# Sorting the first four units in groups of four rows, and the third expert's weights behind the first slots' loads

## Chip, cores and metric

The kernel runs on one core of one Trainium2 chip. The metric is the device time of one execution in microseconds (us). The program is built once; input and output lie in the chip's memory.

## What is computed

A causal depthwise convolution with seven taps per head, softmax-normalised, over 8 x 3584 rows of 192 numbers; then a mixture of eight experts that sends each of the 28,672 rows to its best expert alone.

```python
out = np.einsum('hk,bskhg->bshg', w, x_unf)      # w: softmax of the 7 taps
logits = x @ w_gate                              # x: those 28672 rows
e_idx = np.argmax(logits, axis=1)
eom = 1.0 / (1.0 + np.exp(-(x @ w_output_gate)))
...
h = np.maximum(x[mask] @ w1[e], 0.0)             # 192 -> 1024
ye = h @ w2[e]                                   # 1024 -> 192
out[mask] = gate_w[mask, None] * eom[mask, e, None] * ye
```

## The kernel before

The rows are cut into 16 **units** of 1,792. For each unit `front_a` computes the convolution (PE, line 381, with the matrices `band`), transposes the result (line 404) and takes the logits (line 416, in tiles of 32 columns). `front_b` finds each row's expert on DVE and sorts: the unit is cut into 8 groups of 224 rows (112 on the lower and 112 on the upper block, `l`), and the rows of a group that go to one expert are packed into pieces of `QR` = 2 rows, the last piece of an expert padded. The sorting is a matmul with a selection matrix `pm` (DVE, line 519): four matmuls of line 558 per group write 128 pieces of two rows to PSUM, ACT copies them as fp16 to one of twelve buffers `xs` (line 358, through `evac`), and one indirect DMA of GpSimd, the **scatter** (`scatter`, line 574), writes the 128 pieces of 1 KB to places `du` (line 541) in the DRAM stream `xcg_sorted`, where each expert has its stretch. A group is so one PE step, one ACT copy and one scatter; a unit is eight of them.

The experts run over **slots** of 512 rows of the stream (`Slot`): SP loads a slot with two transposing DMAs, `xa` and `xb` (lines 689 and 691, `slot_load`), PE computes `first` (lines 733 and 741, out to `ht`) and, one slot later, `second` (line 790), ACT scales to `y`, and GpSimd scatters 128 rows a time to the output (line 594). There are 56 planned slots and 5 that choose their expert at run time; a loop behind them takes what is left over.

The weights of expert `e` are four DMAs of GpSimd's queue, cast to fp16 on the way into `wres` (`load_w`, line 339; in this order 256, 64, 64 and 384 KB of fp16). `first` needs the first three of them, `second` the fourth. Experts 0 and 1 are asked for at the start.

The order of the work is written out by hand. In the **fill** a string of letters gives it: `a` to `e` are steps of `front_a` of units 0 to 4, `0` to `3` steps of `front_b` of units 0 to 3, `W` one DMA of the third expert's weights (index 2), `L` the loads of the first three slots (SP's queue) with the four pieces of unit 5's `x`. After each letter the scatters that are ready go to GpSimd's queue. Behind the string come the **stages**, each with three or four slots, one unit's sorting and one unit's convolution, woven together; here experts 3 to 7 are loaded, one DMA at a time, at fixed places. The first slots need the scatters of units 0 and 1 complete. The last eight groups of unit 3 are sorted in the first stage. Slots take the experts in turn, so slot 7 is the first of expert 6 and slot 8 of expert 7.

GpSimd works its queue in order: a scatter, a weight DMA and an output scatter wait for whatever stands ahead.

Of the kernel before, what the change touches and what calls it, by code (L numbers as in the profile page):

```python
# [21 lines left out]
def kernel(  # L22
# [10 lines left out]
    nc = tc.nc  # L33
# [3 lines left out]
    E = moe_w1.shape[0]  # L37
# [35 lines left out]
    xcgq = xcg.rearrange("(a b) w -> a (b w)", b=QR)  # L73
# [165 lines left out]
    nc.vector.tensor_copy(out=hole, in_=rowi[:, 3:4])  # L239
    nc.vector.tensor_scalar(out=hole, in0=hole, scalar1=float(HB), scalar2=-64.0,  # L240
# [24 lines left out]
    NXS = 12  # L265
    xss = [const.tile([128, QR, RW], FP16, name=f"xs{i}") for i in range(NXS)]
    for t in xss:
        nc.gpsimd.memset(t[:, :, XW:RW], 0.0)

    poi = const.tile([128, QR, 128], U32)  # L270
    nc.gpsimd.iota(poi, pattern=[[1, QR], [QR, 128]], base=1, channel_multiplier=0)
    pos16 = const.tile([128, 256], FP16)
    nc.vector.tensor_copy(out=pos16, in_=poi.rearrange("p r j -> p (r j)"))

# [32 lines left out]
    c0 = NB * E  # L307
# [5 lines left out]

# [123 lines left out]
    def front_b(u, split=False):  # L437
        cv, gb = units.pop(u)
        P = slice(0, BP)
        mx = pr.tile([128, NB], FP32, tag="mx", name="mx")  # L440
# [35 lines left out]
        nc.vector.tensor_scalar(out=nu, in0=pn[:, 0:1], scalar1=float(QR - 1), scalar2=None,  # L476
                                op0=ALU.add)
        nc.vector.tensor_scalar(out=nu, in0=nu, scalar1=QR.bit_length() - 1, scalar2=None,
# [19 lines left out]
        nc.tensor.matmul(pk[:, 0:c0], np16, lsum[:, 0:c0], start=False, stop=False)  # L498
        nc.tensor.matmul(pk[:, c0:NK], np16, lsum[:, c0:NK], start=False, stop=True)
# [13 lines left out]
        def prep(i):  # L513
            if cv is not None and i % 2 == 0:
                for k in (i, NG + i):
                    nc.vector.tensor_copy(out=xr[P, k:k + 2, 0:D], in_=cv[P, k:k + 2, :])
            pms[i] = pp16.tile([128, 2, 256], FP16, tag="pm", name="pm")
            for l in range(2):
                nc.vector.tensor_scalar(out=pms[i][P, l, :], in0=pos16[P],  # L519
                                        scalar1=pos[P, l * NG + i:l * NG + i + 1],  # L520
                                        scalar2=None, op0=ALU.is_equal)
# [4 lines left out]
        if split:  # L526
# [10 lines left out]
            scalar=rowf[:, 0:1], in1=dd, op0=ALU.is_le, op1=ALU.mult)  # L537
# [3 lines left out]
        nc.vector.tensor_scalar(out=du, in0=dst, scalar1=rowf[:, 0:1], scalar2=None, op0=ALU.add)  # L541
# [3 lines left out]
        for i in range(NG):  # L545
            if i == 1 and u >= U0 and u != UA:
                v = u if u < UA else u - 1
                plans[v] = plan(v)
            if i + 2 < NG:
                prep(i + 2)  # L550
            while len(pend) >= NXS:
                emit_in()
            xs = xss[nxs[0] % NXS]
            nxs[0] += 1
            ps = pft()
            for r in range(QR):
                for l in range(2):
                    nc.tensor.matmul(ps[:, r * XW:(r + 1) * XW],  # L558
                                     pms[i][P, l, r * 128:(r + 1) * 128],
                                     xr[P, l * NG + i, :],  # L560
                                     start=(r == 0 and l == 0), stop=(r == QR - 1 and l == 1))
# [453 lines left out]
```

## Time and profile before

| | |
|---|---|
| runs | 549.5, 549.5, 551.89 us (median 549.5) |
| profiled execution | 549.7 us, its span 547.7 us |
| busy PE / DVE / ACT / POOL | 512.5 / 370.8 / 390.1 / 400.7 us |
| granted TensorE clock, mean | 0.977 |
| DMA | 91.28 MB, mean 167 GB/s |

The span is what the profile covers; 2.0 us of the execution lie outside it. Busy time is an engine's own; engines work beside one another. Idle time of an engine is listed by what ended it.

### The profile page before, as it was taken

The page shows a single profiled execution, that of the slowest core. Times are in us where ns is not written, and L with a number is a line of the kernel's source. Part 1 is how long each engine was busy: PE and PEld are TensorE (multiplying, and loading weights), DVE is VectorE, ACT ScalarE, POOL GpSimd, SP SyncE. Part 2 cuts the span into 40 slices and gives each one's busy share as a digit, 9 for nine tenths or more (in the row PEclk, how much of TensorE's full clock was granted, in tenths as well). Part 3 has the DMA queues.
Part 4 walks back from the last instruction along what each step waited for, and adds up shares of the span by engine and source line. Part 5 has one row for each costly group of instructions (what it writes and reads, how often), then busy time and mean ns, then how long its engine had stood idle before and what let it go on. Part 6 is the DMA issues. An engine that isn't in the chain of part 4 may idle for free.

```text
span 547.7 us, 16348 instructions
## 1 busy us (share of the span) xinstructions
PE 512.5 (94%) x5718; PEld 355.4 (65%) x5718; DVE 370.8 (68%) x1428; ACT 390.1 (71%) x754; POOL 400.7 (73%) x447
## 2 busy tenths in 40 slices
PE   8999799968999999999999999999999997999990
PEld 3666466745676766767776776777677774666660
DVE  7888768766686958677785867769587752565230
ACT  3897567746777777778777777877777785777750
POOL 8557876778677777777777777777777777777761
PEclk9999799998999999999999999999999999999995
DMA  8997999999987636957667685957373444679610
GB/s 149 288 300 244 172 222 188 204 175 236 194 197 150 180 116 136 213 118 173 173 141 198 141 214 123 199 138 164 100 145 95 119 106 115 143 157 249 206 66 19
DMA packets 154643, 91.28 MB, mean 167 GB/s; under 512 B 104009, under 2 KB 145588, under 8 KB 154560
## 3 DMA queue, kind: packets, MB, share of 16 engines
q1 hardware_dynamic: 127040, 43.76, 40.8%
q0 software_dynamic: 23360, 43.32, 31.8%
q10 hardware_dynamic: 4160, 3.15, 2.0%
q8 instruction: 45, 0.74, 0.6%
q14 instruction: 38, 0.31, 0.2%
HBM read 37.99 MB, written 42.07 MB: 146 GB/s over the span
## 4 chain that ended last, share of the span: by engine, by line
PE 69%; DMA 13%; DVE 5%; ACT 4%; issue 3%; SPq 2%; POOL 2%; POOLq 0%; ACTq 0%; DVEq 0%
PE pyt L790 23%; PE pp L733 17%; PE pp L741 10%; PE pf L381 6%; PE pf L558 6%; PE pf L404 4%; DMA xcg_sorted<-xs,du 4%; PE pf L416 3%; DMA out_dram<-y,oi 3%; DMA xb<-xcg_sorted 3%; DMA wres<-in_moe_w_dram 2%; DMA xt<-in_x_dram 2%; DVE ht L762 1%; POOL xcg_sorted L574 1%; ACT ht L764 1%
## 5 line engine op out<-in xcount | busy, mean ns | idle before, releaser
L594 POOL DMA_INDIRECT out_dram<-y,oi x236 | 234.5, 994 | 77.6 <-issue 40.8
L764 ACT ACTIVATE ht<-pp 128x1024 f16<-128x1024 f32 (+1 forms) x183 | 175.6, 994 | 47.6 <-PE pp L733 38.3
L790 PEld LDWEIGHTS <-ht 128*128 128x128 f16 x1888 | 160.5, 98 | 26.4 <-issue 1.3
L790 PE MATMUL pyt<-wres,ht 128*128 128x192 f16 x1792 | 177.2, 247 | 0.0
L574 POOL DMA_INDIRECT xcg_sorted<-xs,du x128 | 129.1, 1008 | 50.0 <-ACT xs L358 15.4
L762 DVE TENSOR_SCALAR ht<-pp 128x1024 f16<-128x1024 f32 (+1 forms) x61 | 72.5, 1188 | 93.2 <-PE pp L733 91.9
L798 ACT ACTIVATE y<-pyt,g 128x192 f32<-128x192 f32 x236 | 87.0, 424 | 35.2 <-PE pyt L790 27.7
L733 PE MATMUL pp<-xa,wres 128*128 128x512 f16 x224 | 89.2, 398 | 2.5 <-DMA xa<-xcg_sorted 2.5
L733 PE MATMUL pp<-xb,wres 128*128 128x512 f16 x224 | 86.3, 385 | 0.3 <-DMA xb<-xcg_sorted 0.3
L741 PE MATMUL pp<-xb,wres 64*128 64x512 f16 x224 | 70.7, 394 | 12.5 <-DMA wres<-in_moe_w_dram 7.2
L733 PEld LDWEIGHTS <-wres 128*128 128x128 f16 x448 | 41.4, 118 | 56.1 <-issue 31.8
L358 ACT CAST xs<-pf 128x392 f16<-128x392 f32 x128 | 63.2, 509 | 11.3 <-PE pf L558 10.7
L741 PE MATMUL pp<-xa,wres 64*128 64x512 f16 x224 | 70.9, 395 | 0.0
L558 PE MATMUL pf<-xrow,pm 120*128 120x196 f16 x512 | 63.9, 249 | 0.1
L519 DVE TENSOR_SCALAR pm<-pos,pos 120x256 f16<-120x256 f16 x256 | 63.9, 317 | 0.0
L381 PE MATMUL pf<-xt,band 64*64 64x192 f32 x896 | 49.5, 334 | 0.3 <-DMA xt<-in_x_dram 0.3
L358 ACT COPY tt<-pf 128x448 f32<-128x448 f32 x57 | 29.6, 554 | 26.4 <-PE pf L404 24.8
L358 ACT COPY cv<-pf 120x384 f32<-120x384 f32 x84 | 38.3, 508 | 14.0 <-PE pf L381 12.0
L558 PEld LDWEIGHTS <-pm 120*128 120x128 f16 x512 | 44.3, 98 | 4.7 <-DVE pm L519 1.0
L741 PEld LDWEIGHTS <-wres 64*128 64x128 f16 x448 | 17.3, 118 | 42.9 <-issue 33.9
L359 DVE COPY cv<-pf 120x384 f32<-120x384 f32 x44 | 24.4, 554 | 23.8 <-PE pf L381 23.4
L404 PEld LDWEIGHTS pf<-identf,cv 56*128 56x128 f32 x768 | 31.8, 142 | 10.9 <-DVE dd L535 2.6
(161 smaller groups left out, 512.6 us busy)
## 6 DMA issues: line engine op xcount, KB each, us to landing
xt<-in_x_dram SPq DMA_DIRECT2D x39, 384.0 KB
wd<-wres SPq DMA_DIRECT2D x5, 768.0 KB
out_dram<-y,oi POOLq DMA_INDIRECT x236
wres<-in_moe_w_dram POOLq DMA_DIRECT2D x8, 384.0 KB
wres<-in_moe_w_dram POOLq DMA_DIRECT2D x8, 256.0 KB
xcg_sorted<-zrow SPq DMA_DIRECT2D x8, 256.0 KB
xcg_sorted<-xs,du POOLq DMA_INDIRECT x128
xt<-in_x_dram SPq DMA_DIRECT2D x5, 336.0 KB
```

The lines of the kernel that those rows point to most:

```text
L358: return nc.scalar.copy(out=o, in_=i)
L381: nc.tensor.matmul(pcs[g][64 * c:64 * c + 64, o:o + NB // 2 * GH], band[64 * g:64 * g + 64, h + hh, :], xt[64 * g:64 * g + 64, c * NB // 2 ...
L519: nc.vector.tensor_scalar(out=pms[i][P, l, :], in0=pos16[P], scalar1=pos[P, l * NG + i:l * NG + i + 1], scalar2=None, op0=ALU.is_equal)
L558: nc.tensor.matmul(ps[:, r * XW:(r + 1) * XW], pms[i][P, l, r * 128:(r + 1) * 128], xr[P, l * NG + i, :], start=(r == 0 and l == 0), stop= ...
L574: i = nc.gpsimd.indirect_dma_start(out=xcgq, out_offset=bass.IndirectOffsetOnAxis(ap=du[:, i:i + 1], axis=0), in_=xs.rearrange("p r w -> p ...
L594: i = nc.gpsimd.indirect_dma_start(out=out, out_offset=bass.IndirectOffsetOnAxis(ap=oi[:, j:j + 1], axis=0), in_=y[:, j, :], in_offset=Non ...
L733: nc.tensor.matmul(pps[r][:, l, :], w[:, o:o + F // 2].rearrange("p (c q) -> p q c", q=FCH // 2)[:, 2 * q2 + r], x, start=(r == lead), sto ...
L741: nc.tensor.matmul(pps[r][:, l, :], w[p0:p0 + 64, F:WA].rearrange("p (c q) -> p q c", q=FCH // 2)[:, 2 * q2 + r], x[p0:p0 + 64], start=(r ...
L762: nc.vector.tensor_relu(out=ht, in_=pps[r])
L764: nc.scalar.activation(out=ht, in_=pps[r], func=AF.Relu)
L790: nc.tensor.matmul(self.pp[:, o:o + D], self.ht[fc // 2][:, fc % 2, q * 128:(q + 1) * 128], self.w[:, w:w + D], start=(fc == 0 and q % 2 = ...
L798: nc.scalar.activation(out=self.y[:, j, :], in_=self.pp[:, (j - j0) * D:(j - j0 + 1) * D], func=AF.Identity, scale=self.g[:, j:j + 1])
```

## The change

Units 0 to 3 (`u < UQ`) are sorted in pieces of four rows, the others in pieces of two as before. With pieces of four a group has at most 64 pieces, so two groups (`t`) share one buffer pair and one scatter of 128 pieces of 2 KB. In the fill the two groups are computed at once, each in one half of PE's columns, by eight matmuls a group in the place of four; unit 3, which is sorted in the first stage, keeps four matmuls a group, and each group's result is copied in two copies of 64 partitions. `du` takes three DVE instructions for such a unit in the place of one. The twelve buffers become one tile `xsb`. In the string the four `W` move from ahead of the `L` to behind it.

```diff
+    UQ = 4
...
+        q, ls, row = (2 * QR, lsum4, rowq) if u < UQ else (QR, lsum, rowf[:, 0:1])
...
-        nc.vector.tensor_scalar(out=du, in0=dst, scalar1=rowf[:, 0:1], scalar2=None, op0=ALU.add)
+        if q == QR:
+            nc.vector.tensor_scalar(out=du, in0=dst, scalar1=row, scalar2=None, op0=ALU.add)
+        else:
+            for g in range(2):
+                h = slice(64 * g, 64 * g + 64)
+                nc.vector.tensor_scalar(out=du[h, 0:NG // 2],
+                                        in0=dst[h].rearrange("p (t g) -> p g t", g=2)[:, g, :],
+                                        scalar1=row[h], scalar2=None, op0=ALU.add)
+            nc.vector.tensor_scalar(out=du[:, 0:NG // 2], in0=du[:, 0:NG // 2], scalar1=1,
+                                    scalar2=None, op0=ALU.logical_shift_right)
...
+            if fill[0] is None:
...
+                xq = xs[64 * g:64 * g + 64, :, 0:XW].rearrange("p (h r) w -> p r h w", r=2)
+                for r in (g, 1 - g):
+                    w = evac(xq[:, r], ps[64 * r:64 * r + 64, 0:2 * XW].rearrange(
+                        "p (h w) -> p h w", h=2), "dve" if g and r == 0 else "act")
...
+            else:
+                for r in range(2):
+                    for l in range(2):
+                        for j in range(2):
+                            nc.tensor.matmul(
+                                ps[64 * j:64 * j + 64, r * XW:(r + 1) * XW],
+                                pms[2 * t + j][P, l, (2 * g + r) * 64:(2 * g + r + 1) * 64],
+                                xr[P, l * NG + 2 * t + j, :],
+                                start=(r == 0 and l == 0), stop=(r == 1 and l == 1),
+                                tile_position=(0, 64 * j))
+                evac(xs[:, 2 * g:2 * g + 2, 0:XW],
+                     ps[:, 0:2 * XW].rearrange("p (r w) -> p r w", r=2), "act")
+            if g:
+                pend.append(lambda t=t, xs=xs: scatter(u, du[:, t:t + 1], xs, q))
...
-    for k in ("aaaaaaaapXbpab0bb00bb00brb00brcc00101c1c101X0c0ccq1dc1qcd1d2d212"
-              "1d21d1212dWW2Wtdde2We3L2e33223et223"):
+    for k in ("aaaaaaaapXbpab0bb00bb00brb00brcc00101c1c101X0c0ccq1dc1qcd1d2"
+              "d2121d21d1212d2tdde2e3LW2We3W3223Wet223"):
```

GpSimd's queue in the fill, from the last four scatters of unit 1 to the first weight DMA of the first stage (expert 3's, `128x2x512`), before (`xs` are the buffers, `xrow` the unit's two columns of gate weights):

```order
L574 DMA xcg_sorted<-xs_267,du 117504x512
L574 DMA xcg_sorted<-xs_268,du 117504x512
L339 DMA wres<-in_moe_w_dram 128x2x512
L339 DMA wres<-in_moe_w_dram 64x512
L574 DMA xcg_sorted<-xs_269,du 117504x512
L339 DMA wres<-in_moe_w_dram 64x512
L574 DMA xcg_sorted<-xs_270,du 117504x512
L339 DMA wres<-in_moe_w_dram 128x2x768
L574 DMA xcg_sorted<-xs_271,du 117504x512
L491 CAST xrow_257<-gs 120x16
```

and now, the last scatters of unit 1 and the first of unit 2 as `x3`:

```order
L619 DMA xcg_sorted<-xsb,du 58752x1024 x3
L338 DMA wres<-in_moe_w_dram 128x2x512
L619 DMA xcg_sorted<-xsb,du 58752x1024
L338 DMA wres<-in_moe_w_dram 64x512 x2
L491 CAST xrow_259<-gs 120x16
L492 TENSOR_TENSOR xrow_259<-gs,xrow_259 120x16
L619 DMA xcg_sorted<-xsb,du 58752x1024
L338 DMA wres<-in_moe_w_dram 128x2x768
L619 DMA xcg_sorted<-xsb,du 58752x1024
L338 DMA wres<-in_moe_w_dram 128x2x512
```

In the first fence the row ending in `xs_267` is unit 1's last scatter, and four more scatters of unit 2 stand behind the last row shown. On this queue there are half as many scatters, and the four weight DMAs still stand among unit 2's: the first behind two of its groups (before: one), the next two behind four (one and two), the fourth behind six (three). The `L` issues on SP's queue, whose order is the same in both.

PE's queue, the first of unit 0's groups: before, four matmuls for a group,

```order
L416 MATMUL pf<-tt,wg 32x224 x12
L558 LDWEIGHTS pm
L558 MATMUL pf<-xrow_256,pm 128x196
L558 LDWEIGHTS pm
L558 MATMUL pf<-xrow_256,pm 128x196
```

and now eight, in half-width pairs (`64x196`: 64 columns of the array, 196 rows through it):

```order
L415 MATMUL pf<-tt,wg 32x224 x12
L600 LDWEIGHTS pm
L600 MATMUL pf<-xrow_258,pm 64x196
L600 LDWEIGHTS pm
L600 MATMUL pf<-xrow_258,pm 64x196
L600 LDWEIGHTS pm
L600 MATMUL pf<-xrow_258,pm 64x196
```

Each matmul brings its own weight load, so units 0 to 2 issue 192 matmuls and as many loads where they issued 96.

## Rows read from the trace of the kernel before

**Rows 1.** Waits of PE: line, what for, us in total, times, longest.
```profile
PE pp L741 <- DMA wres<-in_moe_w_dram: 7.2, 2, 4.5
```
**Rows 2.** Timeline of PE, 50 to 136 us: start us, us, what, [idle before <-releaser].
```profile
50.22 0.51 PE L558 MATMUL pf<-xrow,pm 120*128 120x196 f16 x4
50.66 1.34 PE L416 MATMUL pf<-tt,wg 128*32 128x224 f32 x24
...
58.51 1.00 PE L558 MATMUL pf<-xrow,pm 120*128 120x196 f16 x8
63.46 0.58 PE L741 MATMUL pp<-xb,wres 64*128 64x512 f16 x1 [3.95 <-DMA xb<-xcg_sorted]
...
72.03 0.38 PE L741 MATMUL pp<-xb,wres 64*128 64x512 f16 x1 [0.95 <-DMA xb<-xcg_sorted]
...
122.28 0.40 PE L741 MATMUL pp<-xb,wres 64*128 64x512 f16 x1 [4.53 <-DMA wres<-in_moe_w_dram]
...
134.63 0.41 PE L741 MATMUL pp<-xb,wres 64*128 64x512 f16 x1 [2.66 <-DMA wres<-in_moe_w_dram]
```
**Rows 3.** Stretches: length, busy PE, PEld, DVE, ACT, POOL, granted clock, DMA share, GB/s.
```profile
50.00:55.00 5.00, 4.48 (x76) 2.67 (x73) 4.42 (x20) 3.15 (x8) 3.78 (x5) 1.00 0.47 174
55.00:60.00 5.00, 4.51 (x62) 2.74 (x58) 4.59 (x21) 4.53 (x14) 4.39 (x6) 1.00 0.76 145
60.00:65.00 5.00, 1.54 (x18) 1.16 (x20) 2.32 (x10) 0.27 (x1) 3.85 (x6) 0.62 1.20 165
...
66.00:68.00 2.00, 2.00 (x10) 1.25 (x9) 1.79 (x14) 1.65 (x2) 1.39 (x3) 0.50 1.13 215
68.00:70.00 2.00, 2.00 (x26) 1.38 (x25) 1.86 (x10) 1.59 (x4) 1.70 (x3) 0.99 1.21 190
...
132.00:134.00 2.00, 0.00 (x0) 0.00 (x0) 0.73 (x4) 0.78 (x3) 1.39 (x3) 1.00 1.15 249
```
**Rows 4.** Timeline of ACT: unit 1's last two copies and unit 2's first.
```profile
48.89 1.38 ACT L358 CAST xs<-pf 128x392 f16<-128x392 f32 x3
```
**Rows 5.** Timeline of POOL, 52 to 115 us.
```profile
52.91 1.53 POOL L574 DMA_INDIRECT xcg_sorted<-xs,du  x1 [0.30 <-issue]
...
55.71 1.33 POOL L339 DMA_DIRECT2D wres<-in_moe_w_dram  x2
...
67.67 0.98 POOL L574 DMA_INDIRECT xcg_sorted<-xs,du  x1 [0.31 <-ACT ht L764]
68.63 0.80 POOL L339 DMA_DIRECT2D wres<-in_moe_w_dram  x1
...
114.35 0.62 POOL L339 DMA_DIRECT2D wres<-in_moe_w_dram  x1
...
```
**Rows 6.** The chain that ended last: start us, us, what.
```profile
52.91 4.43 DMA xcg_sorted<-xs,du
...
74.79 0.34 PE pf L558 x4
```
**Rows 7.** Timeline of SP's queue: the first slot's loads.
```profile
57.76 1.25 SPq L689 DMA_TRANSPOSE xa<-xcg_sorted  x1
```
**Rows 8.** DMA queues at 96 to 102 us: packets, MB, share of 16 engines.
```profile
q1 hardware_dynamic: 1552, 0.87, 86.5%
q0 software_dynamic: 113, 0.16, 29.3%
```
**Rows 9.** Timeline of DVE: unit 1's `du`.
```profile
37.55 0.23 DVE L541 TENSOR_SCALAR du<-dst,rowf 128x8 uint32<-128x8 f32 x1
```
**Rows 10.** The page's groups: out<-in xcount | busy, mean ns of one.
```profile
L594 POOL DMA_INDIRECT out_dram<-y,oi x236 | 234.5, 994 | 77.6 <-issue 40.8
L574 POOL DMA_INDIRECT xcg_sorted<-xs,du x128 | 129.1, 1008 | 50.0 <-ACT xs L358 15.4
L359 DVE COPY cv<-pf 120x384 f32<-120x384 f32 x44 | 24.4, 554 | 23.8 <-PE pf L381 23.4
L558 PEld LDWEIGHTS <-pm 120*128 120x128 f16 x512 | 44.3, 98 | 4.7 <-DVE pm L519 1.0
```

More of the change, by code (lines that the diff above doesn't have):

```diff
@@ L72 @@
     xcg = nc.dram_tensor("xcg_sorted", (E * CAP, RW), FP16, kind="Internal").ap()
-    xcgq = xcg.rearrange("(a b) w -> a (b w)", b=QR)
+    xcgs = {q: xcg.rearrange("(a b) w -> a (b w)", b=q) for q in (QR, 2 * QR)}
     const = ctx.enter_context(tc.tile_pool(name="const", bufs=1))
@@ L239 @@
     nc.vector.tensor_copy(out=hole, in_=rowi[:, 3:4])
+    rowq = const.tile([128, 1], FP32)
+    nc.vector.tensor_scalar(out=rowq, in0=hole, scalar1=2.0, scalar2=None, op0=ALU.mult)
     nc.vector.tensor_scalar(out=hole, in0=hole, scalar1=float(HB), scalar2=-64.0,
@@ L265 @@
     NXS = 12
[L266 to L273, printed above, removed]
+    xsb = const.tile([128, NXS, QR, RW], FP16)
+    nc.gpsimd.memset(xsb[:, :, :, XW:RW], 0.0)
+    pos16 = {}
+    for q in (QR, 2 * QR):
+        poi = const.tile([128, q, 256 // q], U32, name=f"poi{q}")
+        nc.gpsimd.iota(poi, pattern=[[1, q], [q, 256 // q]], base=1, channel_multiplier=0)
+        pos16[q] = const.tile([128, 256], FP16, name=f"pos{q}")
+        nc.vector.tensor_copy(out=pos16[q], in_=poi.rearrange("p r j -> p (r j)"))
     GE = NG * E
@@ L312 @@
     nc.vector.tensor_copy(out=lsum[0:GE, c0 + 2 * NSEG:NK], in_=eqe[:, 0:E])
+    lsum4 = const.tile([128, NK], FP16)
+    nc.vector.tensor_scalar(out=lsum4, in0=lsum, scalar1=2.0, scalar2=None, op0=ALU.mult)
     msks = [const.tile([128, NB + NG, E], FP16, name=f"msk{i}") for i in range(3)]
@@ L475, in front_b @@
         nu = pr.tile([128, 1], U32, tag="nu", name="nu")
-        nc.vector.tensor_scalar(out=nu, in0=pn[:, 0:1], scalar1=float(QR - 1), scalar2=None,
+        nc.vector.tensor_scalar(out=nu, in0=pn[:, 0:1], scalar1=float(q - 1), scalar2=None,
                                 op0=ALU.add)
-        nc.vector.tensor_scalar(out=nu, in0=nu, scalar1=QR.bit_length() - 1, scalar2=None,
+        nc.vector.tensor_scalar(out=nu, in0=nu, scalar1=q.bit_length() - 1, scalar2=None,
                                 op0=ALU.logical_shift_right)
@@ L497, in front_b @@
         nc.tensor.matmul(pk[:, GE:2 * GE], ones16[P, :], mfl[P, 0:GE], start=False, stop=False)
-        nc.tensor.matmul(pk[:, 0:c0], np16, lsum[:, 0:c0], start=False, stop=False)
-        nc.tensor.matmul(pk[:, c0:NK], np16, lsum[:, c0:NK], start=False, stop=True)
+        nc.tensor.matmul(pk[:, 0:c0], np16, ls[:, 0:c0], start=False, stop=False)
+        nc.tensor.matmul(pk[:, c0:NK], np16, ls[:, c0:NK], start=False, stop=True)
         dm = pr.tile([128, NB, E], FP32, tag="dm", name="dm")
@@ L518, in prep @@
             for l in range(2):
-                nc.vector.tensor_scalar(out=pms[i][P, l, :], in0=pos16[P],
+                nc.vector.tensor_scalar(out=pms[i][P, l, :], in0=pos16[q][P],
                                         scalar1=pos[P, l * NG + i:l * NG + i + 1],
@@ L536, in front_b @@
             out=dd, in0=pk[:, c0:c0 + NSEG].rearrange("p (i e) -> p i e", e=E + 1),
-            scalar=rowf[:, 0:1], in1=dd, op0=ALU.is_le, op1=ALU.mult)
+            scalar=row, in1=dd, op0=ALU.is_le, op1=ALU.mult)
         dst = pr.tile([128, NG], FP32, tag="dst", name="dst")
@@ L550, in front_b @@
                 prep(i + 2)
[L551 to L554, printed above, removed]
             ps = pft()
[L556 to L561, printed above, removed]
@@ L562, in front_b @@
-            evac(xs[:, :, 0:XW], ps[:, 0:QR * XW].rearrange("p (r w) -> p r w", r=QR),
-                 "act")
-            pend.append(lambda i=i, xs=xs: scatter(u, du, xs, i))
+            if q == QR:
+                while len(pend) >= NXS:
+                    emit_in()
+                xs = xsb[:, nxs[0] % NXS]
+                nxs[0] += 1
+                for r in range(q):
+                    for l in range(2):
+                        nc.tensor.matmul(ps[:, r * XW:(r + 1) * XW],
+                                         pms[i][P, l, r * 128:(r + 1) * 128],
+                                         xr[P, l * NG + i, :],
+                                         start=(r == 0 and l == 0), stop=(r == 1 and l == 1))
+                evac(xs[:, :, 0:XW], ps[:, 0:2 * XW].rearrange("p (r w) -> p r w", r=2), "act")
+                pend.append(lambda i=i, xs=xs: scatter(u, du[:, i:i + 1], xs, q))
+                yield
+                continue
@@ new lines, in front_b @@
+            t, g = i // 2, i % 2
+            if g == 0:
+                while len(pend) >= NXS // 2:
+                    emit_in()
+                k = nxs[0] % NXS
+                xs = xsb[:, k:k + 2].rearrange("p k r w -> p (k r) w")
+                nxs[0] += 2
+            if fill[0] is None:
+                for h in range(2):
+                    for l in range(2):
+                        nc.tensor.matmul(ps[:, h * XW:(h + 1) * XW],
+                                         pms[i][P, l, h * 128:(h + 1) * 128],
+                                         xr[P, l * NG + i, :],
+                                         start=(h == 0 and l == 0), stop=(h == 1 and l == 1))
+                xq = xs[64 * g:64 * g + 64, :, 0:XW].rearrange("p (h r) w -> p r h w", r=2)
[3 more added lines that the diff above has]
+                    if g:
+                        nodep(w, f"xv{u}_{i}_{r}", (f"xv{u}_{i}_1",) if r == 0 else ())
+            else:
+                for r in range(2):
+                    for l in range(2):
+                        for j in range(2):
[7 more added lines that the diff above has]
+                     ps[:, 0:2 * XW].rearrange("p (r w) -> p r w", r=2), "act")
@@ L565, in front_b @@
+            if g:
+                pend.append(lambda t=t, xs=xs: scatter(u, du[:, t:t + 1], xs, q))
             yield
@@ L571, with scatter @@
     nxs = [0]
-    def scatter(u, du, xs, i):
+    def scatter(u, at, xs, q):
         i = nc.gpsimd.indirect_dma_start(
-            out=xcgq, out_offset=bass.IndirectOffsetOnAxis(ap=du[:, i:i + 1], axis=0),
+            out=xcgs[q], out_offset=bass.IndirectOffsetOnAxis(ap=at, axis=0),
             in_=xs.rearrange("p r w -> p (r w)"), in_offset=None,
-            bounds_check=E * CP - 1, oob_is_err=False)
+            bounds_check=E * CP * QR // q - 1, oob_is_err=False)
         nodep(i, f"sc{u}", [f"sc{v}" for v in range(NU)] + ["load", "guard"])
```

## The prediction

> **What bounds the kernel now.** I read the waits of PE first: once the slots run, PE waits for almost nothing but DMAs, 7.2 us in two waits for expert weights among them [rows 1]. The timeline of PE says where. It ends the fill at 59.51 (58.51 + 1.00), then stands 3.95 us until slot 1's `xb` is there, 0.95 us at slot 2 for the same, 4.53 us at 122.28 (slot 7, expert 6) and 2.66 us at 134.63 (slot 8, expert 7) for weights [rows 2]. Everything behind slot 8 hangs on PE, so what slot 8 starts earlier the end comes earlier.
>
> The stretches say what the first wait costs beside its length: the granted clock is 0.50, the lower level of 1.2 GHz, at 66 to 68 us and back at 0.99 (2.4 GHz) behind 68 [rows 3]. From 63.46 to 68.0 PE works at half rate, which is 2.3 us lost. The 2.66 us wait leaves the clock at 1.00 (132 to 134) [rows 3].
>
> The same rows show DMA: its share is 0.47 and 0.76 at 50 to 55 and 55 to 60, and 1.1 to 1.2 behind 60 (over 1 because the queues overlap) [rows 3]. In the loaded stretch GpSimd's queue q0 and SP's queue q1 push each other aside: when q1 has 86.5%, q0 gets 29.3% and moves 0.16 MB in 6 us [rows 8]. The last weight piece that slot 7 needs is issued at 114.35 and PE starts at 122.28, 7.9 us later, though it is one of the small ones [rows 5, 2].
>
> What lets slot 1 go? Unit 1's last copy ends at 48.89 + 2 x 0.46 = 49.8 [rows 4]. Its scatter starts only at 52.91 with the 0.30 us gap of an engine that has work waiting [rows 5]: GpSimd runs 3.1 us behind. It lands 4.43 us after its start [rows 6], SP issues slot 1's loads at 57.76 [rows 7], and 5.7 us later PE starts.
>
> **The change, part by part.**
>
> *Scatters.* An indirect DMA costs GpSimd 1,008 ns for 1 KB pieces and 994 ns for output rows of 768 bytes [rows 10], so its price goes with the 128 indices and I take the same for 2 KB. With the gap a scatter is 1.3 us. Units 0 and 1 issue 8 in the place of 16 (10.4 us less), so the 3.1 us lag goes; units 2 and 3 save another 4 x 1.3 = 5.2 us each.
>
> *DVE.* `du` takes three instructions in the place of one of 0.23 us [rows 9]: 0.5 us more a unit, 0.9 for units 0 and 1, DVE being busy 4.4 to 4.6 of 5 us there [rows 3]. I put all of it on the path; at the other end none of it is. So unit 1's last scatter starts at 49.8 + 0.9 + 0.3 = 51.0 and not 52.91: **-1.9 us**. With none of it, -2.8.
>
> *Landing.* A scatter now moves 256 KB and not 128. At 174 GB/s [rows 3] the second 128 KB is 0.75 us; the ends are nothing and another full 4.43. DMA is half idle there, so I take **+0.75**.
>
> *Third expert's weights.* They are in GpSimd's queue, the first slots' loads in SP's. The first piece stays ahead of the loads and comes up to 3 us sooner than 55.71 [rows 5], in idle DMA time; two pieces of 64 KB fall behind the loads of slot 1, which at the same rate is **-0.75** for those loads (ends: nothing, and 1.5 for twice that). Slot 3 needs them, 20 us later, so no wait takes this one's place; were they 10 us late it would still be covered.
>
> *PE in the fill.* 96 more matmuls and weight loads. Four matmuls of a group take 0.34 us in the chain [rows 6], 85 ns for 196 rows. The 24 matmuls of line 416, in column tiles of a quarter, move 224 rows each: one after another at that rate they would take 24 x 85 x 224/196 = 2.3 us, and they take 1.34 [rows 2]. So column tiles run beside one another, and two half-width matmuls should take the time of one: nothing. The other end is 0.34 us more a group. The loads, 98 ns each [rows 10], hide beside matmuls as line 416's 24 do.
>
> *Unit 3 in the first stage.* Eight ACT copies become twelve, and DVE gets four. A copy of half the partitions is as long a row: 0.46 us on ACT, 0.55 on DVE [rows 4, 10], 1.8 and 2.2 us more over some 20 us. PE waits for DMA there; taken as nothing, 2 us if DVE's `ht` came late for it.
>
> *Set-up and padding.* Three small DVE instructions and one on GpSimd more, at most 0.3 us each, beside the wait for `x`. Pieces of four pad more: by the reference's argmax over this input the stream grows from 29,196 to 29,432 rows, and the 61 slots still take all of it, the loop behind them nothing. Nothing for both.
>
> *Sum.* Slot 1's data come at 63.46 - 1.9 + 0.75 - 0.75, that is 61.6, and PE, with 0.9 us more of DVE behind its fill, is there at 60.4. It stands 1.2 us, less than the 2.66 that left the clock alone, so the 2.3 us of half rate go too. But slot 2's loads follow slot 1's on SP: its data are 1.9 us earlier, not 4.2, and the 0.95 us wait grows to some 3 (between 2.66, which kept the clock, and 3.95, which did not; what a lower clock took there the waits at slots 7 and 8 would give back). **Slot 2 starts 1.9 us earlier.** From there PE runs into the weights of experts 6 and 7. Their DMAs are limited by the loaded DMA engines, not by when they are issued, so they come as much earlier as the load does. The slot loads move 1.9 us; q0's part, unit 2's last scatter (67.67) and expert 3's first piece (68.63) [rows 5], moves by four scatters, 5.2 us. The idle DMA time to take it is (1.2 - 0.47)/1.2 x 5 + (1.2 - 0.76)/1.2 x 5 = 4.9 us. I take the mean of the two queues, **3.5 us**, between 1.9 and 4.9. The waits at slots 7 and 8 stay about as long as they are. 549.7 - 3.5 = 546.2 for the profiled execution; the median of the runs is 0.2 below it, so **546.0**, own range 544.6 to 547.6.
>
> The tile widths change at each group in the fill. The row of line 416 starts at 50.66 behind full-width matmuls of 50.22 + 0.51 with no idle time marked [rows 2]. The Trainium skill, "TensorEngine Tiling (Array Packing)", section Tiling Modes, says that a change of tiling mode drains the TensorE; this row shows no drain of its own.
>
> **The rivals.**
>
> *More: GpSimd was the limit of the weights.* Eight scatters fewer in units 2 and 3 are 10.4 us of its queue; the 114.35 piece could start near 104 and land in time. For it: GpSimd is busy 3.8 to 4.4 of 5 us before the gaps are counted [rows 3]. Against it: 7.9 us from issue to use, and rows 8. Then both weight waits and a second half-rate stretch go: 1.9 + 4.53 + 2.3 + 2.66 = 11.4, so **538.1**. Chance 0.22.
>
> *Nothing: a drain at each change of tile width.* Its price from rows is an exposed weight load, 98 ns [rows 10], on entering and on leaving each of the 16 groups of units 0 and 1: 3.1 us on the way to the last scatter. That leaves 3.5 - 3.1, **549.1**. Rows 2 show no such gap. Chance 0.17. What speaks for it is the rule of the Trainium skill, "TensorEngine Tiling (Array Packing)", Tiling Modes; by it the change would be worth nothing.
>
> *Slower: the half-width pairs do not overlap.* Place: PE in the fill. Each group then costs 0.34 us more, 16 x 0.34 = 5.4 us ahead of unit 1's last scatter, and less 1.9 that is 3.5 us later: **553.0**. It decides from 0.12 us a group on (1.9/16). The quarter tiles' row is fp32 and speaks against it, but no fp16 half-width pair is in this trace. Chance 0.16.
>
> **How the numbers follow.** Forecast 0.45, rivals 0.22, 0.17, 0.16. About 0.5%, 2.75 us, is what a measurement of this kernel can tell from no change: 546.75 is the border. The forecast's own range lies two thirds below it: 0.31 faster, 0.14 same. With the first rival faster is 0.53; the second and a small part of the third make same 0.33; slower 0.14. The range leaves out half of the first rival and most of the third: 538.5 to 551.5.
>
> **What would show it.** GpSimd reaches unit 1's last scatter within a microsecond of its copy, near 51; SP issues slot 1's loads near 55.9; PE's first wait is 1 to 2 us and the clock stays at 1.00 through 60 to 68; slot 2's wait grows to about 3; the waits for weights at slots 7 and 8 stay, both slots some 3.5 us earlier. It is wrong if the loads of slot 1 are not earlier than 57 (a price on PE or DVE ate the lag), if the eight half-width matmuls of a group take over 0.45 us, or if PE passes slot 7 without a wait, which is the first rival.

## The result and the profile after

The changed kernel takes **545.03 us** (median of 10 runs, 542.94 to 548.02), the kernel before 550.25 us (10 runs, 549.14 to 551.89): a ratio of 0.9904, 95% interval 0.9878 to 0.9931. The forecast was 546.0, faster. The profiled execution took 543.74 us (span 542.0), 6.0 less than that of before.

The start of a slot is the first matmul of line 741 before, 786 after. Read slot by slot, the traces show where the time went (us; e5, e6 and e11 are experiments below):

| slot | before | after | e5 | e6 | e11 |
|---|---|---|---|---|---|
| 1 | 63.46 | 59.69 | 59.78 | 63.75 | 59.37 |
| 2 | 72.03 | 68.56 | 68.08 | 72.04 | 67.01 |
| 3 | 83.08 | 80.07 | 81.17 | 83.72 | 84.78 |
| 7 | 122.28 | 115.71 | 121.08 | 122.88 | 119.70 |
| 8 | 134.63 | 128.76 | 129.46 | 134.18 | 131.88 |
| 9 | 145.31 | 142.13 | 141.66 | 144.87 | 145.04 |
| 17 | 213.20 | 209.62 | 208.64 | 212.77 | 212.35 |
| 47 | 448.80 | 445.22 | 444.25 | 448.45 | 447.98 |
| 49 | 464.34 | 460.28 | 459.22 | 464.57 | 460.23 |
| 61 | 529.15 | 523.64 | 524.25 | 530.20 | 523.60 |

After against before: 3.8 us at slot 1, 5.9 at slot 8, 3.2 at slot 9, 3.6 from slot 17 to 47, 5.5 at the end. The lag of GpSimd is gone. Its timeline (columns as in [rows 5]) and SP's first slot load [rows 7]:

```profile
49.71 0.99 POOL L619 DMA_INDIRECT xcg_sorted<-xsb,du  x1 [0.43 <-DVE dst L539]
...
108.86 0.60 POOL L338 DMA_DIRECT2D wres<-in_moe_w_dram  x1
...
121.83 0.59 POOL L338 DMA_DIRECT2D wres<-in_moe_w_dram  x1
```
```profile
53.77 1.23 SPq L734 DMA_TRANSPOSE xa<-xcg_sorted  x1
```

Unit 1's last scatter starts at 49.71, where it stood at 52.91 [rows 5], and GpSimd now waits for it: 0.43 us, where the gap ahead of a DMA that has work waiting is 0.30. SP issues slot 1's loads 4.0 us sooner. The price of a scatter did not move with its bytes:

```profile
L619 POOL DMA_INDIRECT xcg_sorted<-xsb,du x112 | 111.7, 997 | 68.6 <-ACT xsb L357 29.0
```

997 ns for a mean of 14% more bytes, 1,008 before [rows 10]. The sixteen scatters of 2 KB pieces alone take 0.98 to 1.27 us in GpSimd's timeline, 1.05 on average; the first sixteen of before, of 1 KB pieces, took 0.97 to 1.53, 1.09 on average. PE's timeline, to be held against [rows 2]:

```profile
58.66 1.04 PE L600 MATMUL pf<-xrow,pm 120*64 120x196 f16 x16
...
60.47 0.37 PE L786 MATMUL pp<-xb,wres 64*128 64x512 f16 x1 [0.37 <-ACT xsb L357]
...
63.95 0.37 PE L786 MATMUL pp<-xb,wres 64*128 64x512 f16 x1 [0.51 <-ACT ht L809]
...
67.14 0.85 PE L586 MATMUL pf<-xrow,pm 120*128 120x196 f16 x8 [0.66 <-ACT ht L809]
68.56 0.38 PE L786 MATMUL pp<-xb,wres 64*128 64x512 f16 x1 [0.56 <-DMA xb<-xcg_sorted]
...
115.71 0.40 PE L786 MATMUL pp<-xb,wres 64*128 64x512 f16 x1 [0.80 <-DMA wres<-in_moe_w_dram]
...
128.76 0.61 PE L786 MATMUL pp<-xb,wres 64*128 64x512 f16 x1 [4.93 <-DMA wres<-in_moe_w_dram]
```

The wait of 3.95 us at slot 1 is gone altogether: PE comes out of the fill at 59.69, as late as before (59.51), and now the data are there first. In the place of that wait stand small ones on ScalarE, 0.37 to 0.66 us, which copies unit 3's halves beside `ht`. The 4.53 us at slot 7 became 0.80, and slot 8's 2.66 became 4.93. What the waits cost beside their length is in the stretches (columns as in [rows 3]). Before, behind slot 7 and behind slot 8:

```profile
124.00:128.00 4.00, 4.00 (x30) 2.76 (x30) 3.75 (x19) 3.29 (x6) 3.09 (x5) 0.74 1.20 233
...
134.00:136.00 2.00, 1.37 (x22) 1.03 (x23) 0.19 (x1) 0.23 (x1) 1.70 (x2) 1.00 1.03 245
```

After, behind the fill and around slot 8:

```profile
60.00:65.00 5.00, 3.72 (x43) 2.37 (x42) 4.65 (x24) 3.92 (x8) 3.77 (x4) 1.00 1.22 187
65.00:68.00 3.00, 2.34 (x27) 1.36 (x23) 2.77 (x13) 2.12 (x4) 0.11 (x1) 1.00 1.20 254
...
124.00:128.00 4.00, 0.00 (x0) 0.00 (x0) 0.71 (x4) 0.64 (x2) 3.25 (x4) 0.97 1.23 253
128.00:132.00 4.00, 3.24 (x24) 1.84 (x25) 1.22 (x6) 0.82 (x2) 3.09 (x4) 0.50 1.06 200
132.00:136.00 4.00, 4.00 (x38) 3.33 (x39) 1.36 (x7) 2.90 (x6) 3.08 (x4) 0.68 1.16 227
```

The half rate of 63 to 68 us is gone (1.00), but behind slot 8 the granted clock is 0.50 and 0.68, where it was 1.00 before; the wait at slot 7 had left it at 0.74 before. Between slot 8 and slot 9 PE takes 13.4 us where it took 10.7: 2.7 us of what the weights had won are given back there.

The last 2 us come at the end. Both kernels wait there for the loads of the last stage, which hang on the last unit's scatters. Before:

```profile
463.21 0.41 PE L733 MATMUL pp<-xa,wres 128*128 128x512 f16 x1 [2.52 <-DMA xa<-xcg_sorted]
463.88 0.53 PE L733 MATMUL pp<-xb,wres 128*128 128x512 f16 x1 [0.25 <-DMA xb<-xcg_sorted]
```
```profile
464.00:468.00 4.00, 4.00 (x23) 2.20 (x23) 0.00 (x0) 2.05 (x2) 3.08 (x4) 0.58 0.58 143
```

After:

```profile
458.94 0.41 PE L778 MATMUL pp<-xa,wres 128*128 128x512 f16 x1 [1.83 <-DMA xa<-xcg_sorted]
459.97 0.38 PE L778 MATMUL pp<-xb,wres 128*128 128x512 f16 x1 [0.62 <-DMA xb<-xcg_sorted]
```
```profile
460.00:464.00 4.00, 4.00 (x31) 2.18 (x31) 0.00 (x0) 3.03 (x5) 2.94 (x3) 1.00 0.61 144
```

Before, the clock fell to 0.58 behind a wait of 2.52 us; after, two shorter waits left it at 1.00.

### The profile page after: what moved, and what is told of

It is laid out like the page before. It is cut to its first block, busy times and chain, and to the rows that moved or that the text cites. A ratio compares the mean times of both kernels' runs of the same rounds, so it can differ in the third digit from the quotient of the medians.

```text
span 542.0 us, 16481 instructions
## 1 busy us (share of the span) xinstructions
PE 511.3 (94%) x5814; PEld 355.0 (66%) x5814; DVE 373.1 (69%) x1443; ACT 393.5 (73%) x758; POOL 381.1 (70%) x421
## 4 chain that ended last, share of the span: by engine, by line
PE 79%; DMA 7%; DVE 6%; ACT 3%; issue 1%; POOL 1%; SPq 1%; DVEq 0%; POOLq 0%; ACTq 0%
PE pyt L835 25%; PE pp L778 20%; PE pp L786 11%; PE pf L380 7%; PE pf L568 6%; PE pf L403 3%; PE pf L415 3%; DMA wres<-in_moe_w_dram 3%; DMA out_dram<-y,oi 2%; DMA xb<-xcg_sorted 2%; PE pz L143 2%; ACT tt L357 1%; DVE ht L807 1%; ACT cv L357 1%; DVE pm L519 1%
## 5 line engine op out<-in xcount | busy, mean ns | idle before, releaser
L619 POOL DMA_INDIRECT xcg_sorted<-xsb,du x112 | 111.7, 997 | 68.6 <-ACT xsb L357 29.0
L357 ACT CAST xsb<-pf 128x392 f16<-128x392 f32 (+1 forms) x132 | 65.1, 502 | 13.2 <-PE pf L568 11.5
L568 PE MATMUL pf<-xrow,pm 120*128 120x196 f16 x384 | 48.6, 248 | 0.0
L380 PEld LDWEIGHTS pf<-xt,band 64*64 64x64 f32 x896 | 29.8, 132 | 10.8 <-issue 5.9
```

Of the source, the lines that this page charges most:

```text
L380: nc.tensor.matmul(pcs[g][64 * c:64 * c + 64, o:o + NB // 2 * GH], band[64 * g:64 * g + 64, h + hh, :], xt[64 * g:64 * g + 64, c * NB // 2 ...
L568: nc.tensor.matmul(ps[:, r * XW:(r + 1) * XW], pms[i][P, l, r * 128:(r + 1) * 128], xr[P, l * NG + i, :], start=(r == 0 and l == 0), stop= ...
L619: i = nc.gpsimd.indirect_dma_start(out=xcgs[q], out_offset=bass.IndirectOffsetOnAxis(ap=at, axis=0), in_=xs.rearrange("p r w -> p (r w)"), ...
```

## The experiments

Two theories stood against each other for the stretch up to slot 8. **A**: the order of GpSimd's queue decides when weights land. **D**: the DMA engines, loaded without a break from slot 1's loads on, decide, so that what one transfer gains another loses. Nine of the twelve runs (all but e5, e6 and e11) were on two chips on which every kernel, the one before too (708 to 711 us), took about 700 us. There the engines stood for long stretches, most of them behind 90 us. Of e1, which is the code of before but for the string of the fill:

```profile
PE pf L381 <- issue: 15.9, 28, 1.6
...
PE pf L498 <- issue: 10.8, 2, 5.5
```

"issue" is time in which PE waited for nothing that the profile shows; before has no such entry for PE. I read those runs only for the first 90 us of their traces (e1 not even there, it stood at 60 us already), and their ratios as far as their intervals carry.

**e1 and e6: the new order of the fill alone** (the last part of the diff, in the kernel before).

```
-    for k in ("aaaaaaaapXbpab0bb00bb00brb00brcc00101c1c101X0c0ccq1dc1qcd1d2d212"
-              "1d21d1212dWW2Wtdde2We3L2e33223et223"):
+    for k in ("aaaaaaaapXbpab0bb00bb00brb00brcc00101c1c101X0c0ccq1dc1qcd1d2"
+              "d2121d21d1212d2tdde2e3LW2We3W3223Wet223"):
```

> The kernel before with the new order of the fill alone; all units stay in groups of two rows. Theory A (the gain comes from GpSimd's queue: four instructions fewer in each of units 0 to 3, so the weights of experts 6 and 7 are issued earlier): the number of instructions ahead of expert 6's weights is as before, so the time stays within 1 us of before, and slot 7 starts within 1 us of 122.3. Rival B (the order of weights and slot loads on the DMA engines carries the gain): slot 1 starts 2 us or more earlier and the time falls by 2 to 3 us.

> The kernel of e1 once more (the kernel before with the new order of the fill alone), for the same reason. Theory A: within 1.5 us of before, slot 7 within 1 us of 122.3. Rival B (the order on the DMA engines carries the gain): slot 1 starts 2 us or more earlier and the time falls by 2 to 3 us.

e1 (about 700 us): ratio 0.9999 (0.9961 to 1.0036). e6: 550.89 us, ratio 0.9997 (0.9972 to 1.0022). Its scatter and its two long waits are those of before:

```profile
52.92 1.53 POOL L574 DMA_INDIRECT xcg_sorted<-xs,du  x1 [0.30 <-issue]
```
```profile
63.75 0.59 PE L741 MATMUL pp<-xb,wres 64*128 64x512 f16 x1 [4.00 <-DMA xb<-xcg_sorted]
...
122.88 0.61 PE L741 MATMUL pp<-xb,wres 64*128 64x512 f16 x1 [4.48 <-DMA wres<-in_moe_w_dram]
```

By itself the order is worth nothing. SP issued slot 1's loads at 57.38, 0.4 us sooner, and the data were no earlier.

**e2: the groups of four rows alone** (the same two lines undone in the changed kernel).

> The changed kernel with the old order of the fill; units 0 to 3 in groups of four rows. Theory A: nearly the whole gain stays, 4 to 5.5 us below before; slot 7 starts near 116. Rival B: 2 to 3 us below before, with a wait of 1 us or more at slot 1 that the new order had taken away.

About 700 us; ratio 0.987 (0.9798 to 0.9942), so the gain is there without the order. But the early part of the trace shows what the order is for:

```profile
65.48 0.58 PE L786 MATMUL pp<-xb,wres 64*128 64x512 f16 x1 [2.76 <-DMA xb<-xcg_sorted]
...
76.53 0.38 PE L786 MATMUL pp<-xb,wres 64*128 64x512 f16 x1 [2.93 <-DMA xb<-xcg_sorted]
```

SP issued slot 1's `xb` at 55.33 and PE got it at 65.48. GpSimd had issued two weight pieces at 51.45 and two at 54.81; in the changed kernel it is one at 52.67 and the next two at 57.66. In e2 and in the changed kernel:

```profile
51.45 1.35 POOL L338 DMA_DIRECT2D wres<-in_moe_w_dram  x2
...
54.81 1.31 POOL L338 DMA_DIRECT2D wres<-in_moe_w_dram  x2
```
```profile
52.67 0.94 POOL L338 DMA_DIRECT2D wres<-in_moe_w_dram  x1
...
57.66 1.16 POOL L338 DMA_DIRECT2D wres<-in_moe_w_dram  x2
```

On the same chip, e3 and e4, with the new order, started slot 1 at 61.35 and 60.95 with no wait for a DMA, and slot 2 at 69.90 and 70.11. In these executions, one each, the order is worth 4 us at slot 1 and 6 at slot 2: once GpSimd has no lag, it throws its weights in ahead of the loads. How much of that lasts is open. At slot 3 e2 stands at 87.91, and e3 and e4 at 87.20 and 88.21, after waits of their own (2.70 us for `x`, 5.82 for the slot's load); e10 and e12 below, the changed kernel itself up to there, stand at 83.39 and 81.70 on the other of the two chips. Over the whole time e2's ratio of 0.987 is no worse than the changed kernel's 0.9904, so a gain of the whole kernel from the order is not shown.

**e4, e5 and e9: the weights earlier.** e4 and e5 are one kernel; e9 moves by one position.

```
-                if 12 * (u - U0) + pos in (0, 2, 4, *range(6, 23)):
+                if 12 * (u - U0) + pos in range(20):
```
```
-                if 12 * (u - U0) + pos in (0, 2, 4, *range(6, 23)):
+                if 12 * (u - U0) + pos in (0, 2, *range(4, 22)):
```

> The changed kernel with the 20 weight pieces of the first stages issued one at each of the first 20 positions, instead of at positions 0, 2, 4 and 6 to 22: expert 6's last piece comes three positions earlier, expert 7's too. Theory A (the queue's order decides when weights land): the waits at slots 7 and 8 (0.8 and 4.9 us) and the half rate behind them go, and the kernel is 4 to 7 us faster than the changed one. Rival D (the loaded DMA engines decide): the pieces land no earlier, the wait at slot 8 stays at 3 us or more, or slots 2 to 6 wait for their own loads instead, and the time is within 2 us of the changed kernel's.

> The kernel of e4 once more (the 20 weight pieces of the first stages at the first 20 positions, one each), since on the chip of e1 to e4 all kernels, the one before too, took about 700 us and all engines stood for stretches in which they waited for nothing that the profile shows. Theory A (the queue's order decides when weights land): no wait for weights of over 0.5 us at slots 7 and 8, no half rate at 126 to 136 us, 4 to 7 us faster than the changed kernel, that is 538 to 541 us where before takes 550. Rival D (the loaded DMA engines decide): a wait of 3 us or more at slot 8 or new waits for slot loads at slots 2 to 6, and a time within 2 us of the changed kernel's 545.

> The changed kernel with the weight pieces of the first stages at positions 0, 2 and 4 to 21 instead of 0, 2, 4 and 6 to 22, so that all pieces from the fourth on come one position earlier (e5 had moved them by three). Theory D: what the weights gain the slot loads and the loads of x lose; slot 9 starts within 1 us of 142.1, less at most the 2.7 us that the half rate behind slot 8's wait costs if that wait falls below 3 us: 0 to 2.7 us below the changed kernel's time. Theory A: slots 7 and 8 some 2 us earlier each, with no later start of slots 4 to 6, and 2 to 4 us below.

e4 and e9 (about 700 us): 0.9981 (0.9933 to 1.003) and 0.9888 (0.9798 to 0.9978), which order nothing here; in e4 slot 3 waited 5.82 us for its own load. e5: **545.9 us** (median of four runs), ratio 0.9913 (0.9885 to 0.994), no better than the changed kernel. Its PE:

```profile
106.33 0.86 PE L380 MATMUL pf<-xt,band 64*64 64x192 f32 x10 [2.31 <-DMA xt<-in_x_dram]
...
129.46 0.40 PE L786 MATMUL pp<-xb,wres 64*128 64x512 f16 x1
...
136.30 0.86 PE L380 MATMUL pf<-xt,band 64*64 64x192 f32 x10 [0.99 <-DMA xt<-in_x_dram]
```
```profile
108.00:112.00 4.00, 4.00 (x25) 2.98 (x24) 1.89 (x3) 1.37 (x2) 3.26 (x4) 0.60 1.33 262
```

and, from its chain, the load of `x` that was late at 106.33:

```profile
94.19 12.09 DMA xt<-in_x_dram
```

The weights are in time at slots 7 and 8, the 4.93 us are gone. In their place the loads of x are late by 2.31 and 0.99 us, the clock falls at 108 to 112 instead of 128 to 136, slot 7 starts 5.4 us later than in the changed kernel and slot 9 within 0.5 us of it. That is what D expects; A's 4 to 7 us did not come. It does not show that the DMA engines alone did it: the late load took 12.09 us to land, but SP had also issued that pair of loads at 92.40 and not at 83.85, for they stand behind the slots' loads in its queue. SP's queue is a rival of the DMA engines that no run here separates from them.

**e3 and e7: unit 3 in groups of two rows again** (`UQ = 3`), and **e11: the same with another order at the end**.

```
-    UQ = 4
+    UQ = 3
```

> The changed kernel with unit 3, the first that is sorted beside slots, in groups of two rows again: its eight scatters and its single copies come back, the fill stays. Theory A: GpSimd has four instructions more (four times 1.3 us) ahead of the weights of experts 6 and 7, which come 3 to 5 us later: the kernel is 1.5 to 4 us slower than the changed one, although PE loses no time to unit 3's split copies. Rival C (those copies on ScalarE and VectorE, some 2 us of PE waits in the first stage, cost more than the queue gives back): the same time as the changed kernel or up to 2 us faster.

> The kernel of e3 once more (the changed kernel with unit 3, the first sorted beside slots, in groups of two rows again). Theory A (GpSimd's queue decides): unit 3's four scatters are back ahead of the weights of experts 6 and 7, slot 8 starts 3 to 5 us later than the changed kernel's 128.8, and the time is 1.5 to 4 us above the changed kernel's. Theory D (the DMA engines, loaded without a break from slot 1's loads on, decide; four more instructions with the same bytes move nothing): slot 8 within 1 us of 128.8 and the time within 1 us of the changed kernel's 545. Theory C (unit 3's split copies on ScalarE and VectorE cost more than they bring): slots 2 to 6 start 1 us or more earlier, and the time is 1 to 2 us below the changed kernel's.

> e7 and e10 in one kernel, since their stages are far apart and the trace keeps them so: unit 3 in groups of two rows again (read at slots 2 to 47), and the last unit's scatters ahead of the output scatters of its stage (read from slot 49 on). For slots 2 to 47: theory A (GpSimd's queue) says slot 8 starts 3 to 5 us later than the changed kernel's 128.8 and slot 17 1.5 to 4 us later than its 209.6; theory D (the DMA engines) says both within 1 us; theory C (unit 3's split copies cost more than they bring) says slots 2 to 6 start 1 us or more earlier, and slot 17 up to 2 us earlier. From slot 49 on: theory E (PE sets the end) says that the waits of 1.8 and 0.6 us there go, and the end comes 2 to 4 us earlier against slot 47 than in the changed kernel; rival F (GpSimd, without a break from 420 us on, sets it as much) says slot 49 comes 2 us earlier against slot 47, the end less than 1.5 us. With D and E together 541 to 543 us as the median, where before takes 550 and the changed kernel 545.

e3 and e7 (about 700 us): 0.9893 (0.9844 to 0.9942) and 0.9829 (0.9757 to 0.9902). e11, which has e10's edit too: **542.83 us**, ratio 0.9839 (0.98 to 0.9878). Up to slot 47 it shows unit 3's part:

```profile
67.01 0.38 PE L786 MATMUL pp<-xb,wres 64*128 64x512 f16 x1 [0.48 <-DMA xb<-xcg_sorted]
...
76.57 1.54 PE L380 MATMUL pf<-xt,band 64*64 64x192 f32 x10 [2.55 <-DMA xt<-in_x_dram]
...
131.88 0.61 PE L786 MATMUL pp<-xb,wres 64*128 64x512 f16 x1 [4.05 <-DMA wres<-in_moe_w_dram]
```
```profile
76.00:80.00 4.00, 3.43 (x17) 1.34 (x18) 0.56 (x1) 0.48 (x1) 0.22 (x1) 0.50 1.25 202
```

Slot 2 starts 1.55 us sooner than in the changed kernel (C's first half), 0.32 of them already at slot 1. The changed kernel's waits for ScalarE at 64.80 and 67.14 (0.39 and 0.66 us) are gone. But in both kernels the wait that ends last at slot 2 is the one for `xb`, which SP issued 0.84 us sooner here (60.33 against 61.17), and from slot 1 to slot 2 e5, with four units, took 8.30 us, the changed kernel 8.87, e11 7.64. So unit 3 in fours costs some 0.7 to 1.2 us there, and how much of it the copies are is not shown. Then a load of x is late by 2.55 us and the clock is 0.50; slot 3 comes 4.7 us later, slot 8 3.1, slot 17 2.7. D expected slots 8 and 17 within 1 us, which fails. These are A's numbers, but not A's way. GpSimd's scatters and weights stand in one queue, and the scatter at the head waits for a copy that waits for PE:

```profile
83.88 1.07 POOL L619 DMA_INDIRECT xcg_sorted<-xsb,du  x1 [7.66 <-ACT xsb L357]
```

So one late load of x holds PE, PE holds GpSimd, and GpSimd the weights of slot 8. With `UQ = 3` this load was late at 77 to 79 us in all three traces (2.70, 1.85 and 2.55 us in e3, e7, e11), with four units by 0 (after, e12) to 1.25 us (e9). Why eight smaller scatters delay it was not tried, but the traces show what went ahead of it. From 64 to 72 us GpSimd issued five of unit 3's scatters in e11, of 128 KB, and two of 256 KB in the changed kernel, where the first had waited 3.81 us. At 68 to 72 us the DMA queues (columns as in [rows 8]; `x` is on SP's, q1) show, in the changed kernel and in e11:

```profile
q1 hardware_dynamic: 1151, 0.57, 69.6%
q0 software_dynamic: 338, 0.44, 49.9%
```
```profile
q0 software_dynamic: 498, 0.68, 71.2%
q1 hardware_dynamic: 1009, 0.46, 49.2%
```

This is e2 over again: GpSimd, released earlier, moves its own bytes in the place of SP's. It fits, in one execution; no run tests it. The median (542.83 us, inside the 541 to 543 expected for D and E together, though D's half failed) suggests that a typical run loses less than this profiled one, whose 544.78 us is the longest of its six.

**e10 and e12: the last unit's scatters ahead of the outputs.** e11 has this edit as well.

```
+            if u == UL - 1:
+                return 0 if pos < NG else 2
             if pos < NG:
                 return pos % 2
```

> The changed kernel with another order at the end: in the stage before the last, the 4 output scatters that stood between the last unit's 8 scatters come behind them (none at positions 0 to 7, two at each of 8 to 15). In the changed kernel the last unit's last copy ends at 446.1 and GpSimd reaches its scatter at 452.6, 6.5 us late, so the last scatter comes up to 5 us earlier and the waits at slot 49 (1.8 and 0.6 us) go, with any fall of the clock behind them. Theory E (PE sets the end): the profiled execution is 2 to 4 us shorter than the changed kernel's 543.7. Rival F (GpSimd, which issues without a break from 420 to 526 us, sets the end as much): slot 49 has no wait and starts 2 us earlier, but the end moves by less than 1.5 us.

> The kernel of e10 once more (the changed kernel with the last unit's scatters ahead of the output scatters of its stage; all four first units in groups of four rows), since e10 ran on a chip where all kernels took about 700 us. It differs from e11 by unit 3 alone, and up to slot 47 from the changed kernel by nothing. In e11 slot 17 came 2.7 us later than in the changed kernel, and everything from slot 47 on 2.8 us sooner against slot 47. Theory A (unit 3's four scatters fewer bring the weights of experts 6 and 7 earlier): slots 8 and 17 within 1 us of the changed kernel's 128.8 and 209.6, the profiled execution 540 to 542 us, the median 1 to 3 us below e11's 542.8, that is 540 to 542. Rival G (what slot 17 lost in e11 was one late load of x, and another execution loses as much elsewhere): slot 17 between 210.5 and 213, a median within 1 us of e11's.

Both were on a chip of the 700 us kind: 0.9781 (0.9712 to 0.9849) and 0.9943 (0.9886 to 0.9999). One kernel, twice on the same chip, with intervals that exclude each other, while the medians (702.3 against 710.86 us, 698.26 against 710.35) put them the other way round: ratios from there order nothing closer than some 2%. So what e12 was to decide, whether e11 lost time at slot 17 by unit 3's scatters or by one late load, stays open. The edit at the end is read from e11. The last unit's last scatter, in the changed kernel and in e11:

```profile
452.58 0.97 POOL L619 DMA_INDIRECT xcg_sorted<-xsb,du  x1 [0.30 <-DMA xcg_sorted<-xsb,du]
```
```profile
450.25 0.98 POOL L619 DMA_INDIRECT xcg_sorted<-xsb,du  x1 [0.30 <-issue]
```

In the changed kernel slot 47 starts at 445.22 and its last copy had ended at 446.1 (445.61 + 0.49 on ScalarE): a lag of 6.5 us, the same kind as the one the change removed at the front. In e11, whose slot 47 starts 2.8 us later, the scatter is 2.3 us earlier, and SP issues the last stage's first load at 452.79 and not 455.12. There is no wait left at slot 49, and from slot 47 to 61 e11 takes 75.62 us, the changed kernel 78.42: **2.8 us** less, theory E's amount. From there on F takes a part back. GpSimd now issues without a break from 421.77 to the last output, which starts with work waiting:

```profile
532.28 0.98 POOL L639 DMA_INDIRECT out_dram<-y,oi  x1 [0.31 <-issue]
```

In the changed kernel it started at 530.41, after two waits for ScalarE. From slot 47 to the end of the span e11 is 1.8 us shorter (95.0 against 96.8), between E's 2 to 4 and F's 1.5: PE and GpSimd are nearly even there, and in this execution GpSimd, with work waiting up to its last output, takes back a part of what PE had won.

**e8: fewer bytes.**

```
+            self.mute = mute
...
-                nc.vector.tensor_scalar(out=self.oi, in0=idf, scalar1=float(NOID),
+                nc.vector.tensor_scalar(out=self.oi, in0=idf, scalar1=float(NOID) + self.mute * BIG,
...
-            s = Slot(xabi, w, inv)
+            s = Slot(xabi, w, inv, u < U0 + 2)
```

> The changed kernel without the output rows of slots 1 to 6: their indices get 2 to the 30 added, so the scatter instructions stay on GpSimd and move nothing (24 of 128 rows of 768 bytes, 2.4 MB of the some 15 MB that the DMA engines move between 57 and 129 us). Theory A: the weights of experts 6 and 7 are issued at the same times (108.9 and 121.8) and land as late, so slots 7 and 8 start within 1.5 us of 115.7 and 128.8. Theory D: 2.4 MB at the 220 GB/s of this stretch are 11 us of the DMA engines' time; the weights land sooner, the wait of 4.9 us at slot 8 goes or falls below 1 us, the half rate behind it goes too, and the time is 5 to 9 us below the changed kernel's.

About 700 us, ratio 0.9772 (0.9683 to 0.986). Its trace has no wait for weights, but PE was 11 us late at slot 8 (139.99) for other reasons, so nothing follows. Whether fewer bytes alone bring the weights stays open.

## Why the prediction was right, point by point

- *GpSimd's price and lag.* Right: a scatter costs the same with more bytes, and the lag is gone.
- *DVE +0.9 and landing +0.75 on the path.* Both wrong, and too careful. Unit 1's last scatter started at 49.71, not 51.0, and SP's loads followed 4.1 us behind it (53.77), where they had followed 4.85 us behind the smaller scatter [rows 5, 7]. So slot 1's loads moved by 4.0, not 1.9. Even the ends that cost nothing gave only 2.8: the scatter came 0.4 us sooner than they had it, and of the 0.8 us that the landing took less, 0.5 are GpSimd's own, since the scatter of before was one of its long ones (1.53 us [rows 5], now 0.99). The sign "near 55.9" for SP's loads had left out the forecast's own +0.75.
- *The order of the weights.* Forecast -0.75. Alone it is nothing (e6); with four rows it is worth some 4 us at slot 1 (e2 against e3 and e4, one execution each), and in the whole time nothing that the ratios show. The forecast costed it against the queue of before, not against the one that its own first step makes.
- *Slots 1 and 2.* Forecast a wait of 1.2 us and then one of 3; measured none and 0.56, with slot 2 3.5 us earlier and not 1.9. The clock stayed at 1.00 through 60 to 68, as forecast.
- *Half-width pairs.* Forecast free, wrong if eight took over 0.45 us. The chain of the changed kernel has

```profile
41.88 0.46 PE pf L600 x8
```

 where four took 0.34 [rows 6]: 0.12 us more a group, at the point from which the rival "Slower" was to decide. It did not, since PE was not the limit there: the fill ends 0.18 us later, and its last 16 half-width matmuls take 1.04 us where 8 full ones took 1.00 [rows 2] (0.85 where they run without a gap, at 67.14 after). So the pairs do overlap, and cost some 0.1 us a group. Nor did the rival "Nothing" show: its two exposed weight loads, 0.2 us a group and 3.1 in all, are more than the 0.12 measured, and the scatter that they should have held came 3.2 us sooner. The rule of the Trainium skill, "TensorEngine Tiling (Array Packing)", section Tiling Modes, on which that rival leaned, says that a change of tiling mode drains the engine. This trace shows no drain of its own, though a small one inside the 0.12 us can't be excluded.
- *Unit 3's copies.* Forecast nothing, 2 us at the other end. From slot 1 to slot 2 unit 3 in fours takes 0.7 to 1.2 us more than in twos (e5 and the changed kernel against e11), so it lies between the two. By slot 3 the late load of `x` in e11 has turned the order round.
- *Set-up and padding.* Forecast nothing, and nothing shows: the first scatter starts at 29.19 us, where it started at 29.84, and the 61 slots still take all rows.
- *The weights of experts 6 and 7.* This is the step that failed: "their DMAs are limited by the loaded DMA engines, not by when they are issued", hence 3.5 us. The piece for slot 7 was issued 5.5 us sooner (114.35 to 108.86) and slot 7 started 6.6 sooner; that for slot 8 moved by 5.0 (126.81 to 121.83) and slot 8 by 5.9. So they moved with the queue, and by about the four scatters' 5.2 us that the forecast had averaged away. Yet the rival "More" failed too: the waits did not go but gathered at slot 8, the half rate behind 4.93 us took 2.7 us back, and with all weights in time (e5) loads of `x` were late instead. Whether the DMA engines or the order of the queues bind this stretch stays open, since e5 fits D, e11 does not, and e8 could not tell. What was left at slots 17 to 47 is 3.6 us, the forecast's 3.5, by two errors that cancel: the weights moved more than forecast, and the clock gave part of it back. That agreement is luck.
- *The end.* Not in the forecast: 1.9 us more behind slot 47, from a shorter wait that left the clock alone. e6, with two rows, had 2.98 us and a lower clock there, as before had; e5, with four, 1.79 and 0.57 us, nearly the changed kernel's waits, and yet a lower clock:

```profile
460.00:464.00 4.00, 4.00 (x26) 2.64 (x24) 0.00 (x0) 2.57 (x4) 3.09 (x4) 0.66 0.63 146
```

 So it is partly chance, and most of why the profiled execution (543.74 us) lies 2.5 us below the 546.2 forecast for it. The median, 545.03, is 1.0 below its 546.0.

## What to carry to other kernels

Fewer, larger DMA instructions on a queue that lags pay at once for the transfer at its end, but look at what the queue issues next: released earlier, it may throw other transfers in front of the ones that matter (e2). In the loaded stretch here, moving loads among each other moved the wait (e5); then gather or split waits with an eye on the clock, since a wait of 4.9 us cost 7.6. And search for the same lag in other places: e11 found it at the end of the kernel, and is the fastest of these at 542.83 us (545.03 for the changed kernel, measured on another chip; against before, 0.9839 and 0.9904, whose intervals just touch). The same edit with all four units in fours was only timed on a chip that could not tell.

## What the runs showed that I had not expected

- A wait's length is not all that counts for the clock: behind waits of PE of 2.31 us (e5), 2.52 (before) and 2.55 us (e11) it fell to 0.50 to 0.60, behind one of 2.66 us at slot 8 of before it stayed at 1.00 (134 to 136 us, in the stretches above).
- The same kernel takes 550 us on some chips and 708 to 711 on two others, with the first 60 us nearly alike in most (slot 1 at 59.69 after, at 60.47 to 61.36 in e7, e9, e10), but not in all: slot 1 is at 73.02 in e1 and at 63.75 in e6, the same kernel. What the engines wait for there the profile does not say.
